# Attention in front of two expert layers on one core: transfers merged, weight units later, another order and other PSUM homes

## The chip, the cores and the metric

The kernel runs on one core of a Trainium2 chip. Time is device microseconds (us) of one launch, inputs in HBM, output back to HBM; shorter is better. Besides the plain runs one execution was profiled: its page and trace give the start, length and waits of every instruction on TensorE (PE; PEld is its weight load), VectorE (DVE), ScalarE (ACT), GpSimd (POOL) and on SyncE's queue (SP), from which nearly all transfers are issued.

## The reference

Three layers in a row, all float32 in effect: attention with a memory (4 batches, 8 heads, 576 tokens, 64 columns a head), then two feed-forward layers on the 2304 tokens.

```python
scores = where(causal, -1e9, scale * q @ k.T)
a = softmax(scores);  local = a @ v
q_p = where(q > 0, q, exp(q) - 1) + 1
mem = (q_p @ M_prev) / (q_p @ z_prev + 1e-6)
x = sigmoid(beta) * mem + (1 - sigmoid(beta)) * local   # to [2304, 512]
h = x @ w_in;   x = (h - tanh(h)) @ w_out               # 512 -> 2048 -> 512
h = x @ w_in2;  s = h * softmax(h);  out = (layernorm(s) * g_ln) @ w_out2
```

The weights arrive in 64-bit floats and are turned into pairs of float32 words (a high and a low part) on the chip.

## The kernel before

**Tiling.** Attention works on 16 pairs of heads; pair `p` belongs to batch `p // 4`. For each pair q, k and v are loaded, q and k turned so that the head columns lie on partitions (`q_t`, `k_t`), scores `S` multiplied on TensorE (`s_r` for rows 0 to 511, `s_l` for the last 64 rows of two pairs together), masked and their maximum taken on DVE (`s_max`), exponentiated on ACT (`s_exp`), turned back on TensorE (`a_t`, tiles `T`), copied out by ACT (`a_ev`) and multiplied with v (`a_pv`, tile `X`: 80 matmuls in the trace for an even pair, 120 for an odd one, which also does the last rows of both). The memory part is `f_neg`, `f_r`, `f_add` on POOL, `f_exp` on ACT, `m_mm` on TensorE (tile `R`) and `m_eps`, `m_inv`, `m_mul` on DVE. `x_eps`, `x_inv`, `x_mul`, `x_add` join the parts, `x_tp` turns the result (tile `XT`), `x_ev` copies it to `xs`, and `x_mv` sends it by DMA to `xT`, the input of the first expert layer. A phase of two pairs (one even, one odd) repeats eight times.

**Order.** What each engine does in which order is written out by hand in the table `ORDER` (entries `name:pair:engine:part`); each engine and SP's queue run their own instructions strictly in that order. An entry's `@` gives the PSUM homes that its tile takes: there are four homes of two banks (0 to 3), and TensorE can't write a home until ACT or DVE has emptied it.

**Loads.** `load_q`, `load_k` and `load_v` issue four, four and three DMAs a pair from SP; q has two tiles taking turns (one inside `MZ`, the other `nq`), k two, v three. `load_m` loads the memory matrices of a batch with four DMAs: two of `M_prev` and two of `z_prev`, each for half of the partitions. `x_mv` sends each pair by itself, with one DMA more for the last 64 tokens of each two pairs, and two in place of one where the tokens cross from one half of `xT` to the other.

**Weight units.** The first slice of expert weights is four units of 512 KB. `w_ld` issues a unit's load and `w` does its nine conversion steps (one ACT, five DVE, one POOL, then an ACT and a POOL step), for the pairs named in `UNITS`: 0, 2, 6 and 10. The two first are needed by `h` (matmuls `H` of the first expert layer, placed among the last pairs to fill TensorE), the two others by the matmuls `Y` behind them.

**Behind attention** the expert layers run block by block; TensorE is the engine in front there to the end.

Of the kernel before, what the change touches and what calls it, by code (L numbers as in the profile page):

```python
# [39 lines left out]
class Attention:  # L40
# [342 lines left out]

    def x_mv(self, p):
        b, c = divmod(p, self.HP)
        x, full, S = self.x.pop(p), self.full, self.S
        for xt, t0, a, e in self.xT(b * S, b * S + full):
            self.nc.sync.dma_start(out=xt[:, c, t0 : t0 + e].bitcast(F32), in_=x[:, a : a + e])
        if p % 2:
            tails = x[:, full:].rearrange("p (i w) -> p i w", i=2)  # L390
            for xt, t0, a, e in self.xT(b * S + full, (b + 1) * S):
                self.nc.sync.dma_start(
                    out=xt[:, c - 1 : c + 1, t0 : t0 + e].bitcast(F32), in_=tails[:, :, a : a + e]
                )
        self.done.add(p)
# [139 lines left out]
    def w(self, p, i):  # L535
# [9 lines left out]
        s_exp:0:-:7 s_exp:0:-:6 s_max:1:-:9 load_q:3:s s_r:1:-:3@0 s_r:1:-:2@3 s_r:1:-:1@1 s_max:1:-:8
        f_add:0:- s_max:1:-:6 s_exp:1:-:9 s_exp:0:-:2 s_max:1:-:7 s_max:1:-:2 s_max:1:-:0 a_t:0:-:0@2
        s_max:1:-:1 s_max:1:-:4 s_exp:0:-:5 load_v:0:s s_exp:1:-:8 a_ev:0:a:0 a_t:1:-:4@0 a_ev:1:a:4
        heat:0:-:1@0 a_t:0:-:1@2 s_exp:0:-:0 w:0:-:0 a_t:0:-:2@0 a_ev:0:a:1 s_max:1:-:5 s_max:1:-:3
        m_gate:0:- a_ev:0:a:2 m_mm:0:-@3 s_exp:1:-:1 k_t:2:v a_t:1:-:3@1 load_k:3:s q_t:2:v w_ld:2:-
        f_r:1:p w:0:-:1 m_eps:0:- a_ev:1:a:3 s_r:2:-:2@2 w:0:-:2 f_neg:2:- m_inv:0:- s_exp:1:-:2 w:0:-:3  # L550
        s_max:2:-:5 s_r:2:-:3@0 s_max:2:-:4 f_exp:1:- s_r:2:-:1@1 load_q:4:s s_exp:1:-:5 s_exp:1:-:0
        s_max:2:-:6 a_pv:0:-:2@2 s_max:2:-:2 s_max:2:-:7 q_t:3:v s_exp:2:-:2 s_exp:1:-:4 s_exp:1:-:7
        a_pv:0:-:1 load_v:1:s a_pv:0:-:0 m_mul:0:- load_k:4:s k_t:3:v x_eps:0:- s_max:2:-:0 s_exp:1:-:6
        x_inv:0:- a_t:1:-:1@0 w:0:-:4 f_add:1:- a_ev:1:a:1 x_mul:0:- s_exp:1:-:3 load_v:2:s a_t:1:-:0@3
        s_r:3:-:2@0 f_r:2:p s_max:2:-:1 s_max:2:-:3 a_t:1:-:2@2 a_ev:1:a:0 w:0:-:5 s_max:3:-:5
        s_r:3:-:3@1 f_neg:3:- s_exp:2:-:5 load_k:5:s a_ev:1:a:2 x_add:0:p s_exp:2:-:6 s_max:3:-:4
        x_tp:0:-@3 x_ev:0:v s_max:3:-:7 s_r:3:-:1@2 s_exp:2:-:7 f_exp:2:- s_max:3:-:6 w:0:-:6 s_l:3:-@03
        s_max:3:-:8 s_max:3:-:9 m_mm:1:-@1 m_eps:1:- a_pv:1:-:0@0 s_exp:3:-:6 s_exp:2:-:1 a_pv:1:-:2
        a_pv:1:-:3 q_t:4:v s_max:3:-:2 f_exp:3:- a_pv:1:-:1 k_t:4:v s_exp:2:-:4 s_exp:2:-:0 m_inv:1:-
        s_max:3:-:3 load_q:5:s s_max:3:-:0 m_mul:1:- s_exp:2:-:3 w:0:-:7 f_r:3:p s_exp:3:-:9 x_eps:1:-  # L560
        load_v:3:s a_t:2:-:1@3 s_exp:3:-:8 s_max:3:-:1 a_t:2:-:0@1 f_neg:4:- s_exp:3:-:3 x_inv:1:-
        load_q:6:s x_mul:1:- a_ev:2:a:1 f_add:2:- k_t:5:v s_r:4:-:2@2 a_t:2:-:2@3 s_r:4:-:3@0
        s_max:4:-:5 a_ev:2:a:0 a_ev:2:a:2 a_t:3:-:3@1 s_max:4:-:4 s_exp:3:-:4 s_r:4:-:1@3 w:0:-:8
        s_max:4:-:6 s_max:4:-:7 a_ev:3:a:3 q_t:5:v a_t:3:-:4@2 w:2:-:0 m_mm:2:-@1 s_max:4:-:1 m_eps:2:-
        s_max:4:-:0 w:2:-:1 s_max:4:-:2 a_pv:2:-:2@0 a_pv:2:-:0 a_pv:2:-:1 m_inv:2:- f_exp:4:-
        s_max:4:-:3 s_exp:3:-:1 m_mul:2:- a_ev:3:a:4 load_k:6:s x_eps:2:- w:2:-:2 s_exp:3:-:5
        s_exp:4:-:2 f_add:3:- x_inv:2:- s_exp:3:-:7 a_t:3:-:1@2 s_exp:3:-:0 w:2:-:3 a_ev:3:a:1
        s_exp:3:-:2 x_mul:2:- f_neg:5:- s_l:5:-@31 s_max:5:-:9 s_exp:4:-:3 s_max:5:-:8 x_add:1:p
        a_t:3:-:0@2 x_tp:1:-@0 a_ev:3:a:0 s_r:5:-:2@1 a_t:3:-:2@3 a_ev:3:a:2 f_exp:5:- f_r:4:p x_ev:1:v
        s_max:5:-:4 w_ld:6:- load_k:7:s s_r:5:-:1@2 s_exp:5:-:9 s_max:5:-:5 load_m:4:- s_r:5:-:3@0  # L570
        s_exp:4:-:5 s_max:5:-:1 x_add:2:p f_add:4:- s_exp:4:-:1 x_tp:2:-@3 s_max:5:-:3 x_mv:1:-
        s_max:5:-:2 s_max:5:-:0 m_mm:3:-@1 s_exp:4:-:0 s_exp:4:-:7 x_ev:2:v m_eps:3:- s_exp:5:-:2
        m_inv:3:- s_exp:4:-:6 s_max:5:-:7 load_v:4:s q_t:6:v f_r:5:p a_pv:3:-:1@2 a_pv:3:-:0 a_pv:3:-:2
        a_pv:3:-:3 s_exp:4:-:4 k_t:6:v s_max:5:-:6 s_exp:5:-:7 load_q:7:s s_exp:5:-:5 a_t:4:-:1@3
        m_mul:3:- s_exp:5:-:3 a_t:4:-:2@0 f_neg:6:- x_eps:3:- a_ev:4:a:1 x_inv:3:- x_mv:2:- s_exp:5:-:1
        load_q:8:s x_mul:3:- k_t:7:v s_r:6:-:2@1 a_ev:4:a:2 a_t:4:-:0@3 s_r:6:-:3@2 s_max:6:-:5
        f_add:5:- a_ev:4:a:0 x_mv:0:- s_max:6:-:4 s_r:6:-:1@0 s_max:6:-:6 s_max:6:-:7 s_exp:5:-:6
        q_t:7:v a_t:5:-:4@1 s_max:6:-:1 s_max:6:-:0 s_exp:5:-:4 s_max:6:-:2 w:2:-:4 a_pv:4:-:2@3
        f_exp:6:- s_max:6:-:3 a_pv:4:-:0 a_pv:4:-:1 x_eps:4:- load_k:8:s s_exp:5:-:8 a_t:5:-:3@2
        a_ev:5:a:4 x_inv:4:- load_v:5:s x_mul:4:- s_exp:6:-:2 a_ev:5:a:3 a_t:5:-:1@1 s_exp:5:-:0  # L580
        m_gate:4:- w:2:-:5 a_ev:5:a:1 m_mm:4:-@0 m_eps:4:- m_inv:4:- m_mul:4:- f_neg:7:- s_l:7:-@32
        x_add:3:p s_max:7:-:9 a_t:5:-:2@1 a_t:5:-:0@0 s_exp:6:-:3 x_add:4:p s_max:7:-:8 a_ev:5:a:2
        x_tp:3:-@2 a_ev:5:a:0 x_ev:3:v s_r:7:-:2@1 x_tp:4:-@3 w:2:-:6 f_exp:7:- f_r:6:p s_max:7:-:4
        load_k:9:s s_r:7:-:1@0 x_ev:4:v s_exp:7:-:9 s_max:7:-:5 s_r:7:-:3@2 s_exp:6:-:5 s_max:7:-:1
        f_add:6:- s_exp:6:-:1 s_max:7:-:3 m_mm:5:-@3 s_max:7:-:2 s_max:7:-:0 s_exp:6:-:0 x_mv:3:-
        s_exp:6:-:7 a_pv:5:-:2@1 m_eps:5:- s_exp:7:-:2 s_exp:6:-:6 s_max:7:-:7 a_pv:5:-:0 load_v:6:s
# [65 lines left out]
        x_tp:13:-@3 a_ev:15:a:0 h:0:- x_tp:14:-@1 x_ev:13:v x_ev:14:v m_mm:15:-@3 h:0:- a_pv:15:-:2@0  # L652
        m_eps:15:- a_pv:15:-:0 m_inv:15:- a_pv:15:-:1 a_pv:15:-:3 x_mv:13:- m_mul:15:- x_eps:15:-
        x_inv:15:- h:1:-@1 x_mul:15:- x_add:15:v h:1:- x_mv:14:- h:1:- x_tp:15:-@3 x_ev:15:v x_mv:15:-
        h:1:- h:1:- h:1:- h:0:- h:0:- h:0:- h:0:-
    """


# [719 lines left out]
```

## Time and profile before

| | |
|---|---|
| three runs | 775.02, 776.07, 776.79 us; median 776.07 |
| profiled execution | 775.71 us, of which the span from first to last instruction is 773.8 |
| PE busy | 753.3 us (97% of the span) |
| DVE busy | 553.8 us (72%) |
| ACT, POOL busy | 329.3 us (43%), 342.6 us (44%) |
| granted TensorE clock, mean | 0.990 of full speed |
| packets moved by DMA | 124617, of which 101632 under 512 B |
| stretch 0 to 183 us (attention) | all five engines at work |
| stretch 183 to 774 us (expert layers) | PE busy 587.22 of 591 us |

Shares over the whole span mix the two stretches: what a change inside attention is worth is read in the first 183 us. An engine that is idle there names, behind "<-", what ended its wait.

### The profile page before, as it was taken

The page shows a single profiled execution, that of the slowest core. Times are in us where ns is not written, and L with a number is a line of the kernel's source. Part 1 is how long each engine was busy: PE and PEld are TensorE (multiplying, and loading weights), DVE is VectorE, ACT ScalarE, POOL GpSimd, SP SyncE. Part 2 cuts the span into 40 slices and gives each one's busy share as a digit, 9 for nine tenths or more (in the row PEclk, how much of TensorE's full clock was granted, in tenths as well). Part 3 has the DMA queues.
Part 4 walks back from the last instruction along what each step waited for, and adds up shares of the span by engine and source line. Part 5 has one row for each costly group of instructions (what it writes and reads, how often), then busy time and mean ns, then how long its engine had stood idle before and what let it go on. Part 6 is the DMA issues. An engine that isn't in the chain of part 4 may idle for free.

```text
span 773.8 us, 15949 instructions
## 1 busy us (share of the span) xinstructions
PE 753.3 (97%) x6388; PEld 641.0 (83%) x6388; DVE 553.8 (72%) x1063; ACT 329.3 (43%) x518; POOL 342.6 (44%) x267
## 2 busy tenths in 40 slices
...
GB/s 112 160 131 140 145 124 130 129 84 41 0 82 55 82 54 55 82 55 59 78 55 63 74 55 53 35 75 57 55 28 55 123 137 136 135 97 133 113 137 54
DMA packets 124617, 67.11 MB, mean 87 GB/s; under 512 B 101632, under 2 KB 110592, under 8 KB 124544
## 3 DMA queue, kind: packets, MB, share of 16 engines
...
## 4 chain that ended last, share of the span: by engine, by line
PE 88%; DVE 5%; DMA 2%; ACT 1%; issue 1%; SPq 1%; ACTq 0%; DVEq 0%
PE H L771 25%; PE Y L806 25%; PE H L1000 13%; PE X L514 4%; PE S L408 3%; PE T L241 2%; DVE P L435 1%; DMA nq<-in_q_dram 1%; PE S_L L424 1%; SPq L209 1%; PE R L322 1%; PE O16X L1094 1%; PE O15S L1094 1%; PE O14X L1094 1%; PE O13X L1094 1%
## 5 line engine op out<-in xcount | busy, mean ns | idle before, releaser
L806 PE MATMUL Y<-G,wo 128*128 128x512 f32 (+1 forms) x960 | 205.2, 369 | 0.6 <-DVE G L791 0.2
L806 PEld LDWEIGHTS Y<-G,wo 128*128 128x128 f32 x960 | 174.6, 188 | 26.0 <-issue 1.6
L771 PE MATMUL H<-xh,wi 128*128 128x512 f32 (+1 forms) x640 | 152.0, 370 | 0.0
L954 POOL TENSOR_TENSOR raw<-raw,cva 128x512 f32<-128x512 f32 x48 | 63.1, 1314 | 167.8 <-DVE cva L952 154.2
L771 PEld LDWEIGHTS H<-xh,wi 128*128 128x128 f32 x640 | 117.0, 188 | 15.7
L785 ACT ACTIVATE t<-H 128x1024 f32<-128x1024 f32 (+1 forms) x40 | 37.6, 941 | 132.2 <-PE H L771 131.4
L1000 PE MATMUL H<-w2i,Ys 128*128 128x512 f32 x384 | 89.6, 389 | 0.0
L771 PE MATMUL H<-xT,wi 128*128 128x512 f32 (+1 forms) x320 | 84.7, 368 | 0.0
L1000 PEld LDWEIGHTS H<-w2i,Ys 128*128 128x128 f32 x384 | 72.0, 188 | 14.9
L820 DVE TENSOR_TENSOR yT<-Y,yT 128x512 f32<-128x512 f32 (+3 forms) x105 | 77.2, 788 | 1.4 <-PE Y L806 1.2
L789 ACT CAST G<-t 128x1024 fp32r<-128x1024 f32 (+1 forms) x40 | 38.6, 966 | 90.0 <-DVE t L787 90.0
L791 DVE TENSOR_TENSOR G<-t,G 128x1024 fp32r<-128x1024 f32 (+1 forms) x40 | 45.4, 1136 | 40.9 <-ACT G L789 40.9
L462 ACT ACTIVATE P<-P,mx 128x512 f32<-128x512 f32 (+3 forms) x128 | 65.1, 559 | 12.8 <-DVE mx L435 12.8
L1017 ACT ACTIVATE e<-H,s 128x1024 f32<-128x1024 f32 x18 | 20.1, 1117 | 109.3 <-DVE s L1011 109.3
L787 DVE TENSOR_TENSOR t<-H,t 128x1024 f32<-128x1024 f32 (+1 forms) x40 | 44.6, 1114 | 30.6 <-ACT t L785 30.5
L771 PEld LDWEIGHTS H<-xT,wi 128*128 128x128 f32 x320 | 58.8, 188 | 7.7
L1347 POOL TENSOR_TENSOR Ys<-yT,Ys 128x512 fp32r<-128x512 f32 x16 | 20.8, 1297 | 93.3 <-ACT Ys L1346 80.8
L435 DVE CUSTOM_DVE_ANT_0 P<-S,mask 128x512 f32<-128x512 f32 (+3 forms) x128 | 56.5, 480 | 2.9 <-PE S L408 2.0
L493 ACT COPY pt<-T 128x768 f32<-128x768 f32 (+2 forms) x64 | 51.3, 823 | 12.3 <-PE T L241 12.1
L514 PE MATMUL X<-v,pt 128*64 128x65 f32 x1600 | 50.7, 224 | 0.0
L514 PEld LDWEIGHTS X<-v,pt 128*64 128x64 f32 x1600 | 48.4, 139 | 1.9 <-ACT xh L737 0.4
L408 PE MATMUL S<-kT,qT 64*128 64x384 f32 (+3 forms) x256 | 44.7, 467 | 4.1 <-ACT pt L493 2.8
...
## 6 DMA issues: line engine op xcount, KB each, us to landing
...
```

What stands on the lines that cost most here:

```text
L408: nc.tensor.matmul(s, Q[rows, P * r : P * r + P], K[rows, 0:w], start=True, stop=True, skip_group_check=True,)
L435: self.nc.vector.tensor_tensor_reduce(out=self._block(p, i), in0=s, in1=mask, scale=-0.125, scalar=3.0e38, op0=ALU.add, op1=ALU.min, accum ...
L462: self.nc.scalar.activation(t, t, AF.Exp, bias=self.mx[p][:, i : i + 1], scale=-1.0,)
L493: self.copy(pt, T)
L514: self.nc.tensor.matmul(X[r * D : (r + 1) * D, j, W * c : W * (c + 1)], pt[:, r, D * at : D * (at + 1)], v[:, kb, j], start=kb == 0, stop= ...
L771: nc.tensor.matmul(H[a:z, f], wi[:, wl, c, f * P + a : f * P + z], self.x[n][xl][:, c], start=(count[f] == 0), stop=(count[f] == 3 * KD - ...
L787: nc.vector.tensor_tensor(t, H, t, ALU.subtract)
L791: nc.vector.tensor_tensor(G[:, 1], t, G[:, 0].bitcast(F32), ALU.subtract)
L806: nc.tensor.matmul(Y[d][:, 0:NB], wo[:, wl, f, d * P : (d + 1) * P], G[:, gl, f], start=(i == 0), stop=(i == 3 * KF - 1),)
L820: nc.vector.tensor_tensor(y, src, y, ALU.add)
L954: self.eng.tensor_tensor(w, w, a, ALU.add)
L1000: nc.tensor.matmul(H[:, nh * 512 : (nh + 1) * 512], Y[:, yl, c, :], w2i[:, wl, c, nh * 512 : (nh + 1) * 512], start=(k == 0), stop=(k == 3 ...
```

## The change

`load_m` issues two DMAs in place of four, each over all 128 partitions. `x_ev` puts the results of two pairs in one tile and `x_mv` sends both together (the last two pairs still apart), so that attention's result needs 19 DMAs in place of 28, and the memory matrices 8 in place of 16. There are now two such result tiles, one inside `MZ`, one in a tile `nx` that also holds the first q tile. `UNITS` becomes 4, 8, 12 and 14. `ORDER` is written anew with other homes. All matmuls, DVE, ACT and POOL operations of a pair stay what they were; one more `heat` matmul stands near the start.

```diff
-    UNITS = (0, 2, 6, 10)
+    UNITS = (4, 8, 12, 14)
...
-        x = mz.tile([P, 2048], F32, tag="G", name="xs", bufs=2)
-        self.xs = [x[:, P * NC * i : P * NC * (i + 1)] for i in range(3)]
-        t0, self.gates = t[:, 2 * w : 2 * w + P * NC], t[:, 2 * w + P * NC :]
+        t2 = mz.tile([P, 2048], F32, tag="G", name="nx", bufs=2)
+        self.gates, wx = t[:, 2 * w : 3 * w], 2 * self.S
+        self.xs, t0 = [t[:, 3 * w : 3 * w + wx], t2[:, 0:wx]], t2[:, wx : wx + P * NC]
...
-        for j in range(2):
-            rows = slice(j * D, (j + 1) * D)
-            nc.sync.dma_start(
-                out=t[rows, :, 0:D],
-                in_=self.M[b].rearrange("(c j) d e -> j d c e", j=2)[j],
-            )
-            nc.sync.dma_start(
-                out=t[rows, :, D : D + 1],
-                in_=self.z[b].rearrange("(c j) (d o) -> j d c o", j=2, o=1)[j],
-            )
+        nc.sync.dma_start(
+            out=t[:, :, 0:D], in_=self.M[b].rearrange("(c j) d e -> (j d) c e", j=2)
+        )
+        nc.sync.dma_start(
+            out=t[:, :, D : D + 1], in_=self.z[b].rearrange("(c j) (d o) -> (j d) c o", j=2, o=1)
+        )
...
     def x_mv(self, p):
+
         b, c = divmod(p, self.HP)
-        x, full, S = self.x.pop(p), self.full, self.S
-        for xt, t0, a, e in self.xT(b * S, b * S + full):
-            self.nc.sync.dma_start(out=xt[:, c, t0 : t0 + e].bitcast(F32), in_=x[:, a : a + e])
+        x, full, S = self.x[p // 2], self.full, self.S
+        if p >= self.NP - 2:
+            self._move(x[:, full * (p % 2) :][:, 0:full], b, c, 0, full)
+        elif p % 2:
+            self._move(x[:, 0 : 2 * full], b, c - 1, 0, full)
...
-        load_g:0:- load_q:0:s load_q:1:s load_k:0:a warm:0:- heat:0:-:8@1 k_tp:0:-@0 q_tp:0:-@1
+        load_g:0:- load_k:0:a warm:0:- load_q:0:s load_k:1:s heat:0:-:8@2 q_tp:0:-@1 k_tp:0:-@2
```

Three places of the new order. First SP's queue around the loads of q for pairs 9 and 10 (`nq`, then `MZ` before and `nx` now; `M_prev` and `z_prev` are the memory matrices, `xT` the results). Before:

```order
L165 DMA MZ<-in_M_prev_dram 64x4x64
L169 DMA MZ<-in_z_prev_dram 64x4x1
L165 DMA MZ<-in_M_prev_dram 64x4x64
L169 DMA MZ<-in_z_prev_dram 64x4x1
L187 DMA v_117<-in_v_dram 128x4x64 x2
L191 DMA v_117<-in_v_dram 64x2x64
L388 DMA xT_83<-xs 128x448
L388 DMA xT_84<-xs 128x64
L392 DMA xT_84<-xs 128x2x64
L209 DMA nq<-in_q_dram 32x18x32 x4
L209 DMA MZ<-in_q_dram 32x18x32 x4
L209 DMA k_2235<-in_k_dram 32x18x32 x4
```

and now:

```order
L183 DMA v_114<-in_v_dram 128x4x64 x2
L187 DMA v_114<-in_v_dram 64x2x64
L884 DMA raw<-in_moe_w_in_dram 128x2x512
L205 DMA nq<-in_q_dram 32x18x32 x4
L183 DMA v_117<-in_v_dram 128x4x64 x2
L187 DMA v_117<-in_v_dram 64x2x64
L387 DMA xT_83<-nx 128x2x512
L387 DMA xT_83<-nx 128x2x64
L205 DMA k_1951<-in_k_dram 32x18x32 x4
L205 DMA k_1957<-in_k_dram 32x18x32 x4
L163 DMA MZ<-in_M_prev_dram 128x4x64
L166 DMA MZ<-in_z_prev_dram 128x4x1
```

The load of q for pair 9 stood behind seven DMAs of matrices and results; now it stands behind v and one weight unit, and the two merged ones of each kind follow it.

Second, DVE at the turn from pair 1 to pair 2 (`P` is a score block, `kT` and `qT` the turned k and q, `cva` the weight conversion's scratch tile, `n` the memory divisors of pair 0). Before:

```order
L435 ISA P_1_307,mx_282<-S_1_295,mask 128x256
L435 ISA mx_282 128x1
L274 STREAM_TRANSPOSE kT_406<-k_218 128x576
L274 STREAM_TRANSPOSE qT_424<-MZ 128x576
L938 TENSOR_SCALAR cva<-cva 128x512
L347 TENSOR_SCALAR n_431<-R_388 128x2x4
L941 TENSOR_SCALAR cva<-cva 128x512
L351 RECIPROCAL n_431<-n_431 128x2x4
L945 SCALAR_TENSOR_TENSOR raw<-raw,cva 128x512
L435 ISA P_1_445,mx_444<-S_2_435,mask 128x384
```

and now:

```order
L441 ISA P_1_306,mx_283<-S_3_272,mask 128x512
L441 ISA mx_283 128x1
L270 STREAM_TRANSPOSE kT_308<-k_237 128x576
L441 ISA P_0_338,mx_283<-S_3_272,mask 128x512
L441 ISA mx_283 128x1
L270 STREAM_TRANSPOSE qT_359<-nx 128x576
L441 ISA P_0_338,mx_283<-S_1_329,mask 128x256
L441 ISA mx_283 128x1
L441 ISA P_0_338,mx_283<-S_1_329,mask 128x128
```

The three conversion steps (L938, L941, L945) are gone from here; the turning of k and q for pair 2 stands among the score blocks of pair 1 and no longer behind them.

Third, TensorE near the end of attention, from pair 14's `X` to the first fills `H` of the expert layer. Before, fills stood already ahead of it:

```order
L771 MATMUL H_0_3427<-xh_1550,wi_123 128x512 x4
L241 MATMUL T_0_3436<-ident,P_0_3045 128x64 x8
L241 MATMUL T_0_3436<-ident,P_1_3040 128x64 x8
L241 MATMUL T_4_3457<-ident,PL_9_3198 128x64 x10
L771 MATMUL H_0_3427<-xh_1550,wi_123 128x512 x4
L514 MATMUL X_3474<-v_117,pt_2_3434 64x65 x12
L514 MATMUL X_3474<-v_117,pt_0_3454 64x65 x16
L514 MATMUL X_3474<-v_117,pt_1_3423 64x65 x12
L241 MATMUL T_3_3518<-ident,PL_8_3232 128x64 x10
```

and now:

```order
L318 MATMUL R_3411<-MZ,e_3059 64x65 x16
L520 MATMUL X_3430<-v_117,pt_2_3392 64x65 x12
L520 MATMUL X_3430<-v_117,pt_0_3396 64x65 x16
L520 MATMUL X_3430<-v_117,pt_1_3428 64x65 x12
L237 MATMUL T_4_3486<-ident,PL_9_3202 128x64 x10
L237 MATMUL XT_3500<-ident,xa_3394 128x64 x10
L775 MATMUL H_0_3516<-xh_1874,wi_123 128x512 x4
L237 MATMUL T_3_3525<-ident,PL_8_3204 128x64 x10
```

Of the 48 fill matmuls 24 stood ahead of the last `X` (that of pair 15); now 8 do, and 40 behind it.

## Rows read from the trace of the kernel before

**Rows 1.** Stretches: PE, PEld, DVE, ACT, POOL busy (x instructions); PEclk, DMA share, GB/s

```profile
20.00:40.00 20.00, 17.03 (x308) 12.86 (x308) 16.14 (x50) 15.28 (x28) 11.42 (x8) 0.79 0.94 152
...
80.00:100.00 20.00, 19.75 (x474) 16.23 (x472) 19.60 (x61) 18.92 (x35) 16.64 (x13) 1.00 0.71 132
100.00:120.00 20.00, 14.87 (x325) 11.43 (x323) 12.87 (x47) 12.63 (x23) 11.44 (x9) 0.91 0.64 130
...
183.00:774.00 591.00, 587.22 (x2785) 506.96 (x2784) 408.67 (x602) 188.15 (x269) 217.25 (x157) 1.00 0.24 75
```

**Rows 2.** Waits of DVE, 0 to 182 us: us in total, times, longest

```profile
DVE n L359 <- PE X L514: 10.0, 3, 5.3
DVE qT L274 <- DMA nq<-in_q_dram: 7.3, 2, 5.7
...
DVE cva L938 <- ACT cva L936: 1.8, 1, 1.8
DVE kT L274 <- DMA k<-in_k_dram: 1.7, 1, 1.7
```

**Rows 3.** Timeline, 94 to 112 us: start, us, instruction, [idle before <-releaser]

```profile
93.54 1.24 SPq L165 DMA_DIRECT2D MZ<-in_M_prev_dram  x1
...
101.99 2.23 SPq L209 DMA_DIRECT2D nq<-in_q_dram  x4
...
108.43 0.78 DVE L274 STREAM_TRANSPOSE qT<-nq 128x576 f32<-128x576 f32 x1 [5.72 <-DMA nq<-in_q_dram]
...
110.75 1.35 PE L322 MATMUL R<-MZ,e 64*64 64x65 f32 x32 [5.13 <-issue]
```

**Rows 4.** Waits of SP's queue on semaphores, 20 to 150 us, the two longest

```profile
SPq L187 <- PE T L241: 2.9, 5, 1.6
SPq L388 <- DVE mx L435: 2.1, 2, 1.4
```

**Rows 5.** Issues on SP by line: ns min/median/max, first and last start

```profile
L209 SPq DMA_DIRECT2D k<-in_k_dram x56: 311/496/1327, 14.6 to 132.9; - x56
...
L388 SPq DMA_DIRECT2D xT<-xs x20: 465/594/1580, 56.3 to 183.0; - x20
```

**Rows 6.** Timeline of PE: six of the eight odd pairs' X matmuls

```profile
37.56 3.72 PE L514 MATMUL X<-v,pt 128*64 128x65 f32 x120
...
76.14 3.72 PE L514 MATMUL X<-v,pt 128*64 128x65 f32 x120
94.20 3.72 PE L514 MATMUL X<-v,pt 128*64 128x65 f32 x120
118.90 3.72 PE L514 MATMUL X<-v,pt 128*64 128x65 f32 x120
...
156.31 3.72 PE L514 MATMUL X<-v,pt 128*64 128x65 f32 x120
...
174.94 3.72 PE L514 MATMUL X<-v,pt 128*64 128x65 f32 x120
```

**Rows 7.** Busy time by shorter stretch, columns as in rows 1

```profile
20.00:24.00 4.00, 1.60 (x14) 1.12 (x14) 2.10 (x6) 2.44 (x5) 1.65 (x1) 0.50 1.42 164
24.00:28.00 4.00, 4.00 (x22) 2.27 (x22) 2.10 (x9) 2.25 (x5) 2.39 (x2) 0.50 0.97 155
```

**Rows 8.** Timeline, 20 to 24 us, columns as in rows 3

```profile
21.56 0.66 ACT L936 ACTIVATE cva<-raw 128x512 f32<-128x512 f32 x1 [4.05 <-DMA raw<-in_moe_w_in_dram]
...
22.96 1.65 PE L408 MATMUL S<-kT,qT 64*128 64x384 f32 x4 [2.40 <-ACT pt L493]
```

**Rows 9.** Groups of DVE, 0 to 160 us: slowest and fastest conversion step, busy, mean ns

```profile
L952 DVE SCALAR_TENSOR_TENSOR cva<-raw,cva 128x512 f32<-128x512 uint32 x4 | 4.3, 1064 | 0.0
...
L950 DVE TENSOR_SCALAR cva<-raw 128x512 uint32<-128x512 uint32 x4 | 1.7, 426 | 0.0
```

**Rows 10.** Timeline of the end of attention: a fill, the first Y

```profile
160.85 1.20 PE L771 MATMUL H<-xh,wi 128*128 128x512 f32 x4
...
185.21 7.02 PE L806 MATMUL Y<-G,wo 128*128 128x512 f32 x28 [0.18 <-ACT G L789]
```

More of the change, by code (lines that the diff above doesn't have):

```diff
@@ L377, in x_ev @@
     def x_ev(self, p):
-        n = self.NC - 1 + p % 2
-        x = self.x[p] = self._next(self.xs)[:, 0 : P * n]
+        n, g = self.NC - 1 + p % 2, p // 2
+        if g not in self.x:
+            self.x[g] = self._next(self.xs)
+        x = self.x[g][:, self.full * (p % 2) :][:, 0 : P * n]
         self.copy(
@@ L382, in x_ev, with _move @@
         )
+    def _move(self, x, b, c, lo, hi):
+        x = x.rearrange("p (i w) -> p i w", w=hi - lo)
+        for xt, t0, a, e in self.xT(b * self.S + lo, b * self.S + hi):
+            self.nc.sync.dma_start(
+                out=xt[:, c : c + x.shape[1], t0 : t0 + e].bitcast(F32), in_=x[:, :, a : a + e]
+            )
     def x_mv(self, p):
         b, c = divmod(p, self.HP)
-        x, full, S = self.x.pop(p), self.full, self.S
-        for xt, t0, a, e in self.xT(b * S, b * S + full):
-            self.nc.sync.dma_start(out=xt[:, c, t0 : t0 + e].bitcast(F32), in_=x[:, a : a + e])
-        if p % 2:
[L390 to L395, printed above, removed]
+        x, full, S = self.x[p // 2], self.full, self.S
[3 more added lines that the diff above has]
+            self._move(x[:, 0 : 2 * full], b, c - 1, 0, full)
+        if p % 2:
+            self._move(x[:, 2 * full :], b, c - 1, full, S)
+        self.done.update((p - p % 2, p))
     def s_r(self, p, c):
@@ L545 @@
[L545 to L586, printed above, removed]
@@ L652 @@
[L652 to L655, printed above, removed]
+        load_g:0:- load_k:0:a warm:0:- load_q:0:s load_k:1:s heat:0:-:8@2 q_tp:0:-@1 k_tp:0:-@2
+        g_exp:0:- q_t:0:v k_t:0:a f_r:0:p heat:0:-:1@0 s_r:0:-:3@3 s_r:0:-:2@0 load_q:1:s f_neg:0:-
@@ new lines @@
+        s_max:0:-:6 s_exp:0:-:6 s_r:0:-:1@1 q_tp:1:-@2 s_max:0:-:7 s_exp:0:-:7 k_tp:1:-@3 s_max:0:-:4
+        s_max:0:-:3 s_max:0:-:0 load_m:0:- s_exp:0:-:3 load_k:2:s q_t:1:v k_t:1:a f_neg:1:- s_max:0:-:5
+        s_max:0:-:2 heat:0:-:2@0 s_l:1:-@23 s_exp:0:-:4 g_inv:0:- s_max:0:-:1 s_exp:0:-:5 s_exp:0:-:2
+        s_exp:0:-:0 s_r:1:-:3@0 g_cpy:0:p f_exp:0:- m_gate:0:- s_max:1:-:9 f_add:0:- s_max:1:-:8
+        a_t:0:-:0@1 s_max:1:-:7 k_t:2:v f_exp:1:- load_q:2:s s_exp:0:-:1 a_t:0:-:2@3 s_r:1:-:1@2
@@ new lines @@
+        a_ev:4:a:1 a_pv:4:-:2@2 m_eps:4:- a_pv:4:-:0 load_v:5:s s_max:6:-:3 f_neg:6:- s_max:6:-:1
+        a_pv:4:-:1 s_exp:5:-:5 m_inv:4:- k_t:7:v m_mul:4:- x_eps:4:- s_exp:5:-:4 x_tp:2:-@1 a_t:5:-:4@3
+        s_max:6:-:0 s_exp:5:-:0 x_inv:4:- x_ev:2:v s_exp:6:-:1 f_neg:7:- x_mul:4:- x_mv:1:- s_r:6:-:2@0
+        s_exp:5:-:8 a_ev:5:a:4 s_exp:5:-:3 x_add:3:p a_t:5:-:3@1 s_max:6:-:5 s_r:6:-:3@3 load_q:9:s
+        s_exp:5:-:2 a_t:5:-:0@2 a_ev:5:a:3 s_exp:6:-:0 s_max:6:-:4 f_exp:7:- s_l:7:-@01 load_v:6:s
```

171 lines of the change are left out of this document (102 added, 69 removed).

## The prediction

> **What bounds the kernel now.** The forecast is made against the profiled execution: 775.71 us, a span of 773.8 and 1.9 around it; it lies 0.36 us under the median of the three runs, 776.07, which is nothing beside what follows. I read the stretches first. From 183 us on TensorE is busy 587.22 of 591 us [rows 1]; the diff touches nothing there, so the change is worth what it does to the first 183 us. In an undisturbed part of these, 80 to 100 us, PE is busy 19.75 of 20, DVE 19.60, ACT 18.92, POOL 16.64: four engines nearly full at once, and TensorE and DVE can hardly be packed closer. Two stretches stand out: 20 to 40 us (PE 17.03, DVE 16.14, clock 0.79) and 100 to 120 us (PE 14.87, DVE 12.87, clock 0.91) [rows 1]. So there is little to win in the rhythm and something in the holes.
>
> The waits of DVE name the holes: 7.3 us for a q load, 1.7 for a k load, 1.8 for the first conversion's ACT step; the 10.0 us for X lie at the end of attention, where PE is full of other work [rows 2]. The largest hole, in order: SP issues the memory matrices from 93.54 us on, v and three result transfers behind them, and the four q loads of pair 9 only from 101.99; DVE sits 5.72 us until 108.43, and PE 5.13 us after it [rows 3]. Was SP late because it waited, or because it had too much to issue? Its waits on semaphores between 20 and 150 us begin at 2.9 and 2.1 us, each split over several times [rows 4], while one issue takes about 0.5 us at the middle for k loads and 0.59 for a result, and up to 1.6 [rows 5]. SP has a backlog, and the loads of q stand at its end.
>
> The start is the second place. ACT waits 4.05 us for the first weight unit's load, at 21.56 us, with the copies of T queued behind that; PE waits 2.40 us for such a copy, until 22.96 [rows 8]. In 20 to 24 us PE is busy 1.60 of 4, and the granted clock is at its lower level, 0.50, there and from 24 to 28 [rows 7].
>
> The rhythm itself I measure from one odd pair's X to the next: starts at 37.56, 76.14, 94.20, 118.90, 156.31, 174.94 [rows 6]. That is 38.58 us for two phases, then 18.06, 24.70, then 37.41 for two, and 18.63 for the last, which also holds 24 fill matmuls. An undisturbed phase is 18.06 to 18.7.
>
> **The change part by part.**
>
> *Fewer issues.* The code gives 8 in place of 16 DMAs for the matrices and 19 in place of 28 for the results: 17 fewer. A merged one might cost SP more than each of its halves; a k load of 72 KB took 0.50 us at the median and a result of mostly 256 KB 0.59 [rows 5], so size adds little, and I count 0.5 to 0.6 each: 8.5 to 10 us of SP's time over the stage, with the queue's order changed so that q for pair 9 no longer stands behind seven of them. SP's backlog is paid back then, and I expect the two disturbed parts to become ordinary phases: 24.70 to 18.6, 6.1 us, and 38.58 to 37.4, 1.2 us. **Term 1: 7.3 us less.** Bounds: 3 us, if half of the 5.72 us wait stays; 10.4 us, if all six phases between 37.56 and 156.31 (118.75 us) take 18.06. I choose near the ordinary phase because PE, at 19.75 of 20, has nothing else to give there. What is late next is PE itself.
>
> Here the Trainium skill speaks against the change. DMA: Bandwidth & Descriptors, section "Anatomy of one DMA — SWDGE (gpsimd) path", says that the fixed cost of a DMA is mostly its completion, with some 50 ns for the sequencer's dispatch. It describes another queue than SP's; but by that price 17 issues are worth 0.85 us (an estimate from the page), and term 1 would be close to nothing. Rows 5 say half a microsecond, and the sum goes by them.
>
> *Weight units later.* Two edits in one. At the start, the ACT wait of 4.05 us and the conversion's DVE steps leave the first 40 us; the load of 512 KB leaves SP and the DMA engines, whose share was 1.42 and 0.97 from 20 to 28 us [rows 7] (above 1 because packets overlap). What is late next there: k and q for pair 2, which DVE takes a few operations earlier than before, so a wait like the 1.7 us for k [rows 2] may stay. The gain lies between zero (loads take the cover's place) and the sum of PE's wait, 2.40, half of PE's 5.60 busy us at the half clock, 2.80, and one unit's DVE steps: five steps, from 1.7 to 4.3 us for four units [rows 9], about 3.7 us a unit taking the mean of the ends; 8.9 in all. The nearest rows are the wait and the clock, 5.2 us; I take off a part for the loads. **Term 2: 4.5 us less.**
>
> At the end, units of pairs 12 and 14 are converted after the last scores, 7.4 us of DVE work out of the full stretch into one where DVE waits anyway, 10.0 us for X [rows 2]. I cost this at nothing in the middle, as PE is as full as DVE there. But the fills move too: 24 of 48 stood ahead of pair 15's X, now 8 do. A group of four took 1.20 us [rows 10], so 16 matmuls, 4.8 us, no longer fill TensorE's gaps between transposes and copies. PE's work isn't changed by that; what counts is how many of these gaps stay open. Cover is there: the conversions of the last unit, the tanh and the copy that the first Y needs stand in the shadow of the 40 fills behind X, 12 us, where before PE came to Y at 185.21 with a wait of 0.18 [rows 10]. ACT's copies, on which the last transposes hang, are the work that could be late. **Term 3: 1.5 us more**, between 0 (all gaps closed) and 4.8 (all open).
>
> *Homes and order.* Each home must be emptied before TensorE writes it again. The new order does the same work a phase, with the turned k and q earlier and R behind the two transposes of the next pair. No row shows what its waits are. Bounds: zero, as PE was 19.75 of 20 full with the old homes and the new ones can't win more there than term 1's upper bound holds; and, on the other side, one wait per phase like the 2.40 us that PE spent on a copy [rows 8], 16.8 us for seven phases. I take zero, since the clean stretch [rows 1] shows that four homes can carry this amount of work, and keep the other end as a rival. The extra heat matmul lies in a wait for loads and costs nothing; if the cover were gone, 0.3 us, a quarter of a group of four larger ones [rows 10].
>
> **Sum:** 775.71 - 7.3 - 4.5 + 1.5 = 765.4 us; I say 765.5. With the terms' own bounds but not all at once: 760 to 771.
>
> **The rivals.**
>
> *Landing, not issuing (771.2).* Merged DMAs move the same packets; if q comes late because its packets take long, not because SP is behind, the hole at 108 us and its like come back elsewhere, and only term 2 stays, with term 3 at nothing: 775.71 - 4.5 = 771.2. For it: the share of the DMA engines is 0.94 in 20 to 40 us [rows 1]. Against it: it is 0.64 where the largest hole lies [rows 1], and SP began to issue those q loads at 101.99 us, when DVE was 0.7 us from needing them (108.43 less its wait of 5.72, [rows 3]).
>
> The Trainium skill's price of 50 ns, by the section named above, leads to the same 771.2, as by it fewer issues bring nothing; rows 5 are against it, which is why this case gets less than the forecast.
>
> *Slower: a home not empty (782.2).* One place decides: TensorE's first transpose of the next pair needs the home that R held, which DVE frees with `m_mul` behind a row of score blocks and the turned q. If PE waits there as long as it did for a copy, 2.40 us [rows 8], in each of seven phases, 16.8 us come on top: 775.71 - 10.3 + 16.8 = 782.2. It turns the sign from 10.3 / 7 = 1.5 us a phase on. For it: DVE is 98% busy, so any order in which PE hangs on its last operation has no slack. Against it: the same dependence existed with the old homes, and PE's share was 19.75.
>
> *Every phase at its best (756.4).* Six phases of 18.06 us, 10.4 us, and the whole of term 2's bound, 8.9: 775.71 - 19.3 = 756.4.
>
> *Nothing (775.7).* The wait for q goes but an ACT copy or a DVE turn ends last in the same phases, and the start fills with waits for k: the holes change their names.
>
> **How the numbers follow.** Forecast 0.60, landing 0.15, home not empty 0.12, best phases 0.08, nothing 0.05. A difference under 0.2%, 1.6 us, is about what a measurement of this kernel can't tell from none. Faster: the forecast, most of landing, and the best case, less what of these and of the nothing case falls near 775: 0.80. Same: 0.07. Slower: 0.13. The predicted time is the forecast's, 765.5. The range leaves out the slower rival and the nothing case (0.17) and the outermost edge of the best one: 757 to 774.
>
> **What would show it.** Term 1: no wait of DVE for a q load above 1 us after 40 us, and odd pairs' X 18 to 19 us apart throughout; PE's clock at 1.00 around 110 us. Term 2: no ACT wait for a weight unit before 30 us, the first odd X at 32 to 34 us in place of 37.56. Term 3: PE busy above 18.5 of 20 in the last 20 us before the first Y. It is wrong if X stands further apart than 19 us in phases without a DMA wait (then the homes), if q waits stay (then landing), or if the first Y waits for a weight unit.

## The result, and the profile after

The changed kernel takes 765.2 us (median of four runs, 765.0 to 766.9) against 776.4 for the kernel before on the same chip (775.0 to 778.0): a ratio of 0.986, 95% interval 0.984 to 0.988, 11.2 us less. The forecast was 765.5, with a range of 757 to 774. The profiled execution is the longest of the four, 766.86 us with a span of 765.0; its details are 1.7 us dearer than the median.

First the stretches, which answer to rows 1 (columns: PE, PEld, DVE, ACT, POOL busy with instructions, PEclk, DMA share, GB/s):

```profile
20.00:40.00 20.00, 19.99 (x482) 15.80 (x480) 18.66 (x70) 18.86 (x35) 14.55 (x11) 1.00 0.69 119
80.00:100.00 20.00, 18.42 (x452) 15.09 (x452) 17.30 (x59) 17.72 (x32) 13.93 (x11) 1.00 0.85 156
100.00:120.00 20.00, 18.19 (x445) 14.79 (x443) 18.20 (x60) 18.34 (x34) 18.34 (x13) 0.99 0.65 128
120.00:140.00 20.00, 19.97 (x454) 15.85 (x452) 17.76 (x59) 18.02 (x32) 16.87 (x12) 0.93 0.78 194
```

Both holes are gone: PE is busy 19.99 us in 20 to 40 us (17.03 before) and 18.19 in 100 to 120 (14.87). But in 80 to 100 us it has lost, 18.42 against 19.75. DVE's waits, as in rows 2, from 0 to 182 us:

```profile
DVE kT L270 <- DMA k<-in_k_dram: 3.3, 3, 1.9
DVE P L441 <- PE S L414: 3.1, 2, 2.2
DVE n L355 <- PE X L520: 2.6, 6, 0.8
```

The 7.3 us for q are no longer there; 3.3 us for k have taken the place of 1.7. In 80 to 100 us there is a new wait: the program has two result tiles in place of three and fills one again only when it is sent. DVE waited 1.77 us for that, and PE 1.51 us for DVE (b_merge and a_wold below, with the same tiles, have no such wait):

```profile
93.72 0.69 DVE L378 COPY nx<-XT 128x512 f32<-128x512 f32 x1 [1.77 <-DMA xT<-nx]
94.47 0.92 PE L414 MATMUL S<-kT,qT 64*128 64x256 f32 x8 [1.51 <-DVE nx L378]
```

Then the odd pairs' X, as in rows 6 (of eight), and the first Y, as in rows 10:

```profile
32.90 3.72 PE L520 MATMUL X<-v,pt 128*64 128x65 f32 x120
...
107.10 3.72 PE L520 MATMUL X<-v,pt 128*64 128x65 f32 x120
128.29 3.72 PE L520 MATMUL X<-v,pt 128*64 128x65 f32 x120
145.73 3.72 PE L520 MATMUL X<-v,pt 128*64 128x65 f32 x120
161.03 3.72 PE L520 MATMUL X<-v,pt 128*64 128x65 f32 x120
176.10 1.19 PE L810 MATMUL Y<-G,wo 128*128 128x512 f32 x4 [0.98 <-ACT G L793]
178.02 10.54 PE L810 MATMUL Y<-G,wo 128*128 128x512 f32 x44 [0.72 <-DVE G L795]
```

These rows cut the span into four pieces: the start (up to the first odd X), six phases (to the seventh), the last phase (to the eighth) and the rest. The table does so for the profiled execution of each run; the names are those of the experiments below. b_merge_w has no row: its profiled execution ran at a mean granted clock of 0.65 and took 1063 us, so its parts can't be compared.

| kernel | span | start | six phases | last phase | rest |
|---|---|---|---|---|---|
| before | 773.8 | 37.56 | 118.75 | 18.63 | 598.9 |
| changed | 765.0 | 32.90 | 112.83 | 15.30 | 604.0 |
| b_merge | 766.0 | 34.91 | 113.46 | 18.64 | 599.0 |
| b_mpool | 766.1 | 33.66 | 114.55 | 18.63 | 599.3 |
| b_w | 779.3 | 33.53 | 121.80 | 19.06 | 604.9 |
| a_split | 771.4 | 33.85 | 119.08 | 14.24 | 604.2 |
| a_msplit | 772.6 | 33.35 | 119.32 | 15.37 | 604.6 |
| a_mpool | 764.8 | 32.32 | 112.50 | 14.24 | 605.7 |
| a_wold | 768.8 | 36.22 | 116.83 | 14.23 | 601.5 |
| a_old | 773.0 | 37.83 | 119.18 | 14.61 | 601.4 |
| a_h | 768.0 | 32.88 | 112.20 | 18.82 | 604.1 |
| a_even | 765.7 | 33.01 | 116.99 | 14.23 | 601.5 |
| a_tanh | 761.7 | 33.10 | 111.35 | 15.30 | 602.0 |

So of the 8.8 us by which the profiled spans differ (the medians differ by 11.2) the start gave 4.66 (forecast 4.5), the phases 5.92 (forecast 7.3), and last phase and rest together took 1.78 back (forecast 1.5). How far such a piece varies by itself can be read from three kernels that are the same up to the seventh X (changed, a_h, a_tanh): their starts lie within 0.22 us of each other, their six phases at 112.83, 112.20 and 111.35. A difference of phases below some 1.5 us between two profiled executions is therefore no finding.

### The profile page after: what moved, and what is told of

The parts are those of the page before. It is cut to its first block, busy times and chain, and to the rows that moved or that the text cites. A ratio compares the mean times of both kernels' runs of the same rounds, so it can differ in the third digit from the quotient of the medians.

```text
span 765.0 us, 15923 instructions
## 1 busy us (share of the span) xinstructions
PE 749.5 (98%) x6390; PEld 638.5 (83%) x6390; DVE 553.4 (72%) x1063; ACT 329.8 (43%) x518; POOL 343.9 (45%) x267
## 4 chain that ended last, share of the span: by engine, by line
PE 90%; DVE 4%; DMA 3%; SPq 1%; ACT 1%; issue 1%; POOL 0%; DVEq 0%; ACTq 0%
PE Y L810 26%; PE H L775 25%; PE H L1004 13%; PE S L414 4%; PE X L520 4%; PE T L237 2%; PE R L318 1%; PE S_L L430 1%; DMA nx<-in_q_dram 1%; DMA k<-in_k_dram 1%; DVE P L441 1%; SPq L205 1%; PE O16X L1098 1%; PE O15S L1098 1%; PE O14X L1098 1%
## 5 line engine op out<-in xcount | busy, mean ns | idle before, releaser
L441 DVE CUSTOM_DVE_ANT_0 P<-S,mask 128x256 f32<-128x256 f32 (+3 forms) x128 | 56.4, 477 | 3.4 <-PE S L414 3.1
L414 PE MATMUL S<-kT,qT 64*128 64x128 f32 (+3 forms) x256 | 45.9, 468 | 1.9 <-DVE nx L378 1.5
```

The source lines that it names most:

```text
L414: nc.tensor.matmul(s, Q[rows, P * r : P * r + P], K[rows, 0:w], start=True, stop=True, skip_group_check=True,)
L441: self.nc.vector.tensor_tensor_reduce(out=self._block(p, i), in0=s, in1=mask, scale=-0.125, scalar=3.0e38, op0=ALU.add, op1=ALU.min, accum ...
```

## The experiments

Each kernel is one edit away from a kernel already known. The first group asks whether term 1, fewer issues on SP's queue, is real, and whether it is issuing or landing.

**b_merge**: the merges alone. The diff is against the changed kernel, whose units and whole order are put back to the old ones.

```diff
-    UNITS = (4, 8, 12, 14)
+    UNITS = (0, 2, 6, 10)
...
-        load_g:0:- load_k:0:a warm:0:- load_q:0:s load_k:1:s heat:0:-:8@2 q_tp:0:-@1 k_tp:0:-@2
+        load_g:0:- load_q:0:s load_q:1:s load_k:0:a warm:0:- heat:0:-:8@1 k_tp:0:-@0 q_tp:0:-@1
...
```

> The kernel before, with its own order, homes and weight units, and only the two merges of transfers: two DMAs for the matrices of a batch in place of four, the results of two pairs sent together (17 issues fewer, with the new result tiles). Theory 'fewer issues' (term 1 as predicted): the queue of SP is shorter by 8.5 to 10 us, the waits for q near 108 us shrink, and most of the 7.3 us come: 769 to 771 us. Rival 'place in the queue': the loads of q and k for the next pair still stand behind the matrices and results, so the hole stays near 100 to 110 us, 774 to 777 us. Rival 'landing': no change, 776.

768.8 us, ratio 0.990 (0.987 to 0.993): 7.6 us less, just beyond the 769 to 771 of 'fewer issues'. Term 1 has its size. But 2.65 us of it came at the start, which the forecast had given to the weight units. SP's and ACT's rows of that kernel tell part of why:

```profile
14.74 1.80 SPq L880 DMA_DIRECT2D raw<-in_moe_w_in_dram  x1
...
20.38 0.69 ACT L936 ACTIVATE cva<-raw 128x512 f32<-128x512 f32 x1
```

The first unit's load stood behind the memory matrices, too. With two issues fewer ahead of it SP begins it at 14.74 us, and ACT's step at 20.38 has no wait; before, the load was issued at 16.72, and ACT waited 4.05 us until 21.56 [rows 8]. The earlier load is not all of it: ACT also came to the step later here, its last work ahead of it ending at 20.45 us and not at 17.50. PE's granted clock, 0.50 from 20 to 28 us before [rows 7], is 1.00 in b_merge.

**b_mpool**: the kernel before; its 16 matrix transfers, unmerged, are issued from POOL's queue.

```diff
-            nc.sync.dma_start(
+            nc.gpsimd.dma_start(
                 out=t[rows, :, 0:D],
...
-            nc.sync.dma_start(
+            nc.gpsimd.dma_start(
                 out=t[rows, :, D : D + 1],
```

> The kernel before with one edit: the 16 transfers of the memory matrices, four a batch and unmerged, are issued from POOL's queue in place of SP's. As many transfers and bytes as before; only SP has 16 issues less, about as many as the change saves it. Theory 'SP's issuing': as the two merges alone gave (768.8 us), 767 to 771, with the waits for q near 108 us gone. Rival 'number of transfers and their landing': nothing is gained, 775 to 777. Slower, if POOL, 11 to 17 of 20 us busy, becomes late by issuing: 778 or more.

768.0 us, ratio 0.989 (0.988 to 0.991), 8.3 us less, with as many transfers as before. One issue holds POOL about as long as it held SP (0.65 us at the median against 0.62 for the matrices), and the transfers land later, in 4.4 us at the median against 2.6 from SP, and still the time falls. The rows of the kernel before, and then of b_mpool:

```profile
L165 SPq DMA_DIRECT2D MZ<-in_M_prev_dram x8: 605/619/1544, 7.1 to 135.6; - x8
...
DMA to landing us min/median/max: 2.3/2.6/5.1
```

```profile
L165 POOL DMA_DIRECT2D MZ<-in_M_prev_dram x8: 615/648/838, 3.5 to 130.3; - x8
...
DMA to landing us min/median/max: 3.5/4.4/5.4
```

That decides against "landing": what was short was SP's time.

**a_split**: the changed kernel with all 17 issues put back. **a_msplit**: with the matrices' 8 alone. **a_mpool**: with its 8 matrix transfers issued from POOL, 8 fewer on SP.

For the first two `load_m` is that of the kernel before, and a_split changes `x_mv` too:

```diff
-        if p >= self.NP - 2:
-            self._move(x[:, full * (p % 2) :][:, 0:full], b, c, 0, full)
-        elif p % 2:
-            self._move(x[:, 0 : 2 * full], b, c - 1, 0, full)
+        for i in (p - 1, p) if p % 2 and p < self.NP - 2 else (p,) if p >= self.NP - 2 else ():
+            self._move(x[:, full * (i % 2) :][:, 0:full], b, i % self.HP, 0, full)
```

The third changes both transfers of `load_m`:

```diff
-        nc.sync.dma_start(
+        nc.gpsimd.dma_start(
             out=t[:, :, 0:D], in_=self.M[b].rearrange("(c j) d e -> (j d) c e", j=2)
```

> The changed kernel, with the transfers split again at the same places of its queue: four DMAs for the matrices of a batch, and each pair's result by a DMA of its own (17 issues more, same bytes). Theory 'fewer issues': 17 issues of 0.5 to 0.6 us lengthen SP's queue by 8.5 to 10 us, and most of term 1 is lost: 771 to 773 us. Rival 'place in the queue': what counts is what stands ahead of q and k, and the new order has slack for 17 more: 765 to 767. By the price of 50 ns an issue, 766.

> The changed kernel with the matrices' transfers alone split again: 8 issues more on SP, the results stay merged. The 17 of both made it 8.1 us slower, 8 fewer gained nothing. 'Each issue has its price' (straight line): half, 768 to 770. Rival 'a knee' (the new order has slack for a few issues, and only beyond it each counts): 765 to 767. Rival 'it is the results, not the matrices': also 765 to 767.

> The changed kernel with one edit: its 8 merged transfers of the memory matrices are issued from POOL's queue. SP's queue, which has no gap until 139 us in the changed kernel, has 8 issues less, 0.51 us each at the least and 0.67 by the mean of all its issues: 4 to 5 us. Theory 'SP's queue is still the bound of the phases': 760 to 763 us, phases between odd pairs' X shorter by 0.5 to 0.8 us each. Rival 'TensorE and DVE bound the phases now': 764 to 766.

17 more issues: 773.3 us, ratio to before 0.996 (0.994 to 0.998), 8.1 more than the changed kernel. 8 more: 770.3, ratio 0.992 (0.990 to 0.995), 5.1 more, nearest to the straight line. 8 fewer: 767.2, ratio 0.989 (0.987 to 0.990), no gain; the 2.0 us more are within the intervals, and both forecasts were lower. Per issue that is 0.45 (b_merge), 0.48 (a_split) and 0.64 us (a_msplit, where 8 issues and intervals of some 2 us leave 0.3 to either side). DVE's waits for k go the same way, 3.3 us in the changed kernel, 6.6 in a_msplit (in an execution 4.0 us above its median) and 7.3 in a_split (0 to 165 us):

```profile
DVE kT L274 <- DMA k<-in_k_dram: 7.3, 4, 3.3
```

In a_mpool no wait of DVE for q or k is left between 40 and 165 us. Its phases are no shorter all the same, 112.50 against 112.83. That does not show that issues are worth nothing from here on: the fifth phase, where the changed kernel waits for k, is 18.49 us and not 21.19, but the second is 21.95 and not 18.13. POOL, DVE and PE there, and then POOL and DVE at the same step in the changed kernel:

```profile
51.03 0.75 POOL L166 DMA_DIRECT2D MZ<-in_z_prev_dram  x1
51.80 2.79 POOL L300 TENSOR_TENSOR e<-e,fw 128x576 f32<-128x576 f32 x2
51.95 2.93 DVE L942 TENSOR_SCALAR cva<-cva 128x512 f32<-128x512 f32 x1
...
56.21 0.71 PE L237 MATMUL T<-ident,P 64*128 64x64 f32 x16 [2.16 <-DVE mx L441]
```

```profile
53.02 1.42 POOL L300 TENSOR_TENSOR e<-e,fw 128x576 f32<-128x576 f32 x1 [1.98 <-ACT e L296]
...
54.17 0.56 DVE L942 TENSOR_SCALAR cva<-cva 128x512 f32<-128x512 f32 x1
```

In a_mpool two additions on POOL (L300) follow its two issues back to back, and the conversion step on DVE beside them takes 2.93 us in place of 0.56. In both kernels the step ends 0.29 us after POOL's addition; that it waited for POOL is likely from this, but was not tested. PE then waits 2.16 us for DVE and runs at a granted clock of 0.50 from 58 to 60 us. What 8 issues fewer are worth, without work put on POOL for it, stays open.

The second group asks for the weight units, order and homes.

**b_w**: the kernel before with the units alone later. **a_wold**: the changed kernel with the units early. **a_old**: only order and homes of the change (a_split with early units). **b_merge_w**: all but order and homes. The entries `w` and `w_ld` were put at the places that they have, counted in DVE's operations, in the other kernel. For b_w and b_merge_w (the other way round for a_wold and a_old):

```diff
-    UNITS = (0, 2, 6, 10)
+    UNITS = (4, 8, 12, 14)
```

> The kernel before, with its own order, homes and transfers, and only the weight units later: for pairs 4, 8, 12 and 14, at the places among DVE's operations at which the changed kernel has them. Term 2 as predicted: 4.5 us less at the start, first odd pair's X at 33 us; the tail loses little, since 24 fills still stand ahead of the last X, but the last unit is now converted behind it and the first Y can wait 1 to 3 us for it: 772 to 774 us. Rival (the start is bound by loads of k and q anyway): first X at 36 to 37.5, 776 us or more.

> The changed kernel, with the weight units early again (pairs 0, 2, 6 and 10, at the places among DVE's operations at which the kernel before has them); the order of all else, the homes and the merged transfers stay new. Term 2 as predicted: first odd pair's X back at 36 to 38 us, 4.5 us more at the start, and up to 1.5 us less at the tail: 768 to 770 us. Rival (the new order, with k and q turned earlier, covers the unit's wait by itself): within 1 us of the changed kernel, 765 to 766.

> The changed kernel with the transfers split again and the weight units early again: of the change only order and homes are left. As predicted (order and homes worth nothing): 775 to 777.5, as the kernel before. Rival 'the new order itself gains, by turning k and q earlier': 768 to 773. Rival 'a home not empty' (the slower case of the prediction, up to 16.8 us): 780 or more.

> The kernel before, its own order and homes, with both other parts of the change: the merged transfers and the weight units later. It differs from the changed kernel in order and homes alone. As predicted (order and homes worth nothing): 764.5 to 767, as the changed kernel's 765.2. Rival 'the parts don't add' (later units alone made the old order 4 us slower, with unmerged transfers: 780.5): the old order pays at its tail, where the first Y waited 4.1 us for G, what the start gains: 769 to 773, and the new order is then worth 4 us or more.

b_w: 780.5 us, ratio 1.005 (1.003 to 1.007), slower, where 772 to 774 was expected. a_wold: 770.5, 0.991 (0.989 to 0.994), just above its forecast. a_old: 775.8, 1.000 (0.998 to 1.001), as forecast. b_merge_w: 773.5, 0.996 (0.995 to 0.998), where 764.5 to 767 was forecast and 769 to 773 if the parts don't add. With the others, medians in us:

| | units early, split | units early, merged | units late, split | units late, merged |
|---|---|---|---|---|
| old order and homes | 776.4 | 768.8 | 780.5 | 773.5 |
| new order and homes | 775.8 | 770.5 | 773.3 | 765.2 |

The merges are worth 5.3 to 8.1 us everywhere. Order and homes are worth nothing with early units (0.6 less, 1.7 more), and 7.2 and 8.3 us with late ones. Late units cost 4.1 and 4.7 us in the old order and bring 2.5 and 5.3 in the new. The parts don't add. (The intervals are some 2 us wide to either side, so a difference below that is undecided.) Two things stay open. Order and homes were never tested apart. And late units in the old order were tried at one set of places only, taken over from the other kernel, so that the 7 to 8 us hold against those places and not against the best that the old order allows.

Where b_w loses, the table says: the start is 4.03 us shorter, as forecast, but the phases are 3.05 longer (its waits for q are 10.3 us) and last phase and rest 6.5. Its rows around the first Y:

```profile
184.78 0.65 ACT L956 CAST wo<-raw 128x512 fp32r<-128x512 f32 x1 [8.36 <-POOL raw L949]
185.34 1.02 ACT L780 ACTIVATE t<-H 128x1024 f32<-128x1024 f32 x1
...
188.99 11.30 PE L801 MATMUL Y<-G,wo 128*128 128x512 f32 x37 [4.13 <-ACT G L784]
```

ACT sits 8.36 us in the unit's next-to-last step, waiting for POOL, and the tanh on which G and the first Y hang is queued behind it. PE then waits 4.13 us and goes on at a lower clock, by the stretches of that kernel:

```profile
190.00:195.00 5.00, 5.00 (x14) 3.67 (x13) 3.03 (x4) 3.39 (x5) 5.00 (x4) 0.56 0.01 2
```

Where the 8.3 us of b_merge_w lie was not seen; b_w makes the same tail likely, but that was not shown.

The third group asks what the tail costs.

**a_h**: three groups of four fills from behind the last X to places ahead of it. **a_even**: the units' steps spread evenly, all done ahead of the last X; the loads of three units are issued earlier with them. **a_tanh**: the first fill block's last group and its tanh ahead of the last unit's last three steps.

Entries of `ORDER` in a_h, and then in a_tanh:

```diff
-        a_t:15:-:3@0
+        a_t:15:-:3@0 h:0:-
...
-        a_t:15:-:1@2
+        a_t:15:-:1@2 h:0:-
...
-        m_mm:15:-@3
+        m_mm:15:-@3 h:0:-
...
-        w:14:-:3 h:0:- h:0:- h:0:- w:14:-:4
+        w:14:-:3 w:14:-:4
```

```diff
-        w:14:-:5 w:14:-:6 w:14:-:7 w:14:-:8 x_mv:14:- x_mv:15:- h:0:- h:0:- h:1:-@0
+        w:14:-:5 h:0:- h:0:- w:14:-:6 w:14:-:7 w:14:-:8 x_mv:14:- x_mv:15:- h:1:-@0
```

> The changed kernel with three groups of four fill matmuls moved from behind the last X to places among pair 15's transposes ahead of it; nothing else. Term 3 as predicted (16 fills no longer fill TensorE's gaps; 1.5 us lost): part of that comes back, 764 to 765 us, with the last X later by 2 to 3.6 us and the way from it to the end shorter by more. Rival (the gaps are not what the tail costs; the conversions of the last two units are): no gain, 765 to 767.

> The changed kernel with the steps of its four weight units spread evenly over the same stretch, from where pair 4's begin to just ahead of the first fill; the units of pairs 8, 12 and 14 are so converted earlier, the last one before the last X instead of behind it. Rival to term 3 (late conversions cost the tail, as the run with early units, 3.6 us shorter from the seventh odd X to the end, makes likely): tail 2.5 to 3.6 us shorter, phases longer by 0 to 2: 762 to 765 us. Term 3 as predicted (conversions free, fills cost): 765 to 768, since the phases get the steps.

> The changed kernel with one edit in its tail: the last group of the first fill block and its tanh stand ahead of the last three conversion steps of the last weight unit, so that ACT no longer waits 3.1 us for POOL's sum of the weights (at 171.9 us) before it may do the tanh that the first Y needs. If late conversions cost the tail by blocking ACT: TensorE's waits of 1.0 and 0.7 us for G go, 763 to 764.5 us. Rival (the first Y is bound by TensorE's fills or by the unit itself): 765 to 766.5.

a_h: 767.9 us, ratio 0.988 (0.987 to 0.990), 2.7 more than the changed kernel and above both forecasts. Its last phase is longer by 3.5 us, about the time of its 12 fills (3.6 us by rows 10), and behind the last X nothing is saved:

```profile
163.90 3.72 PE L520 MATMUL X<-v,pt 128*64 128x65 f32 x120
178.95 1.20 PE L805 MATMUL Y<-G,wo 128*128 128x512 f32 x4 [1.10 <-ACT G L788]
```

15.05 us from X to Y, against 15.07 in the changed kernel: that way is not set by PE's work but by what G waits for. a_even: 768.1 us, 0.989 (0.988 to 0.991). Its last phase and rest are 3.6 us shorter, just those of a_wold, and PE comes to Y with no wait; but the phases are 4.2 us longer, as far as one execution tells. At neither place was the conversion free: among the phases it cost the phases (whether by its steps or by its earlier loads was not tested), at the end it cost the tail.

a_tanh is the version that beats both: 762.7 us (761.8 to 763.5), ratio to before 0.982 (0.979 to 0.984), just below its forecast. ACT around the last unit in the changed kernel, and then in a_tanh:

```profile
171.89 0.65 ACT L965 CAST wo<-raw 128x512 fp32r<-128x512 f32 x1 [3.06 <-POOL raw L958]
172.44 1.02 ACT L789 ACTIVATE t<-H 128x1024 f32<-128x1024 f32 x1
```

```profile
168.43 1.03 ACT L784 ACTIVATE t<-H 128x1024 f32<-128x1024 f32 x1 [0.44 <-PE H L770]
...
171.05 0.65 ACT L960 CAST wo<-raw 128x512 fp32r<-128x512 f32 x1 [1.59 <-POOL raw L953]
171.61 1.05 ACT L788 CAST G<-t 128x1024 fp32r<-128x1024 f32 x1
...
173.68 8.67 PE L805 MATMUL Y<-G,wo 128*128 128x512 f32 x36
```

The tanh uses the 3 us that ACT spent waiting for POOL, and Y starts with no wait, where the changed kernel had 0.98 and 0.72. Last phase and rest fall by 2.0 us. (Its phases, 1.5 us shorter, lie ahead of the edit.)

## Why the prediction was right, and where it was not

**Term 1** (7.3 us less) was right in cause, and in size over the whole kernel: 7.6 by b_merge, 8.1 by a_split, 8.3 by b_mpool. The step "SP has a backlog" holds, and rows 5's half microsecond an issue is what one was worth: 0.45 to 0.64. The price of 50 ns for an issue's dispatch from the Trainium skill, DMA: Bandwidth & Descriptors, section "Anatomy of one DMA — SWDGE (gpsimd) path", gives for 17 issues an estimate of 0.85 us, a ninth of what was measured. Even on the path that this page of the Trainium skill describes, POOL's queue in b_mpool, one issue held its engine for 0.615 us or more. That a DMA's fixed cost is mostly completion, as the same section of the Trainium skill says, agrees with b_mpool (0.65 us of issue, 4.4 to landing), but is no measure for a queue that only issues. Two steps of term 1 failed. Its place: the forecast took all 7.3 us from the phases, and these gave 5.29 in b_merge and 5.92 in the changed kernel; 2.65 us of the merges' gain lay at the start. And "what is late next is PE itself". The two disturbed parts did become ordinary, 24.70 to 19.13 us and 38.58 to 37.25, which is 6.9 of the 7.3; but next is a k load, in the phase from 107.10 to 128.29, which took 21.19 us and not 18.82 as before. SP, DVE and PE there, and then the stretches:

```profile
110.68 6.59 SPq L205 DMA_DIRECT2D k<-in_k_dram  x8
...
117.17 0.78 DVE L270 STREAM_TRANSPOSE kT<-k 128x576 f32<-128x576 f32 x1 [1.25 <-DMA k<-in_k_dram]
...
118.68 0.53 PE L237 MATMUL XT<-ident,xa 64*128 64x64 f32 x10 [1.81 <-DVE n L355]
```

```profile
118.00:120.00 2.00, 1.32 (x17) 0.94 (x19) 2.00 (x8) 0.40 (x2) 1.09 (x1) 0.88 0.86 140
120.00:122.00 2.00, 2.00 (x16) 1.22 (x14) 1.66 (x5) 1.28 (x3) 1.88 (x2) 0.50 0.86 179
122.00:124.00 2.00, 2.00 (x26) 1.23 (x26) 1.47 (x5) 0.96 (x2) 1.00 (x1) 0.76 0.68 205
```

DVE waits 1.25 us for k, PE 1.81 for DVE, and from there to 124 us PE runs partly at 0.50, the lower of its two levels. A second new wait, foreseen as little, is the one for the result tile that ends at 94.47 us.

**Term 2** (4.5 us less at the start) was right in size, 4.66, and half right in cause. Late units alone are worth 3.3 us (a_wold against the changed kernel) to 4.0 (b_w, and a_split against a_old) there; merges alone take 2.65 of the same hole. The two overlap, and the sum counted the hole once, in the term where it stood nearest. What the step left out is that late units need an order to go with them: in the old one, at the places tried, they cost 4.1 us.

**Term 3** (1.5 us more at the tail) had its size right, 1.78, and its mechanism wrong. It charged the fills moved behind X and held the late conversions free. In a_h the fills fill no gap: 12 of them put back ahead of X make the last phase longer by 3.5 us, their own time, and shorten nothing behind it. By a_wold and a_even the late conversions cost 3.6 us in last phase and rest, so that all else there in the new order, the fills among it, is worth 1.8 the other way (617.5 us before, 615.7 in these two). That the sum of the two is near 1.5 is luck. The failed step is "I cost this at nothing in the middle": it looked at DVE's steps and not at ACT's two, which stand in the same queue as the tanh; a_tanh shows that 2.0 us of the cost were this. The cover fell with it: the tanh that the first Y needs did not lie in the shadow of the fills, and Y waited 0.98 us.

**Homes and order at zero** holds with early units, 775.8 against 776.0 (a_old), and fails with late ones, where they are worth 7 to 8 us. Along one path, order first, then merges, then units, the parts measured 0.6, 5.3 and 5.3 us less. The forecast's 10.3 met 11.2 in the medians and 8.8 in the profiled executions, with two of its terms shifted; that the median came within 0.3 us of the forecast is in part luck.

**The rivals.** "Landing" (771.2) is out by b_mpool. "A home not empty" (782.2) is out by a_old. "Every phase at its best" needed 108.4 us for six phases; the shortest here were 111.35 (a_tanh). "Nothing" is out by the result.

**The signs named beforehand.** No q wait above 1 us, no ACT wait for a unit before 30 us, the first odd X at 32.90, the clock at 1.00 from 106 to 112 us, PE 19.02 of the last 20 us before Y: all held. "Odd X 18 to 19 us apart throughout" did not: the six phases lie between 17.44 and 21.19 us. The longest three of them hold a wait of DVE for a transfer (k, k and the result tile), so they don't speak for the homes. And "wrong if the first Y waits for a weight unit" came true by a detour: Y waited for G, whose tanh stood in ACT's queue behind the unit's step.

A slip of naming: the q loads that the text on the order and the prediction call pair 9's and 10's are those of pairs 11 and 12 (the sixth load into `nq`, and the one behind it). No number depends on it.
